# A windowed attention with a gated MLP on one core: idle products on TensorE in the first stages, the rms weights loaded first, batch 0's value copies on POOL

## The chip, the core and the metric

The kernel runs on one core of a Trainium2 chip. The metric is the device time of one execution in microseconds (us). Five engines work side by side, each in order on its own list of instructions, and wait for each other by semaphores: TensorE (PE in the rows, its weight loads PEld), VectorE (DVE), ScalarE (ACT), GpSimd (POOL) and SyncE (SP), which issues most of the DMAs. TensorE reads SBUF and writes PSUM; its clock has two levels, 1.2 and 2.4 GHz, and the rows give the granted share of it as PEclk (0.50 or 1.00).

## The reference

Attention in a window of 64 positions over 8 batches, 8 heads, 576 positions and 64 channels, and then a gated MLP on the 4608 tokens that come out of it (512 channels, 1536 hidden).

```python
scores = matmul(q, k.T) / sqrt(64)          # per batch and head
mask = (rel >= 0) & (rel < 64)              # rel = query position - key position
scores = where(mask, scores, -1e9) - max(...)
attn = exp(scores) / (sum(exp(scores)) + 1e-9)
x = matmul(attn, v)                         # -> 4608 tokens x 512 channels
rms = sqrt(mean(x * x) + 1e-6)
xn = x / rms * rms_g
g, val = xn @ w_gate, xn @ w_val
out = (g * sigmoid(g) * val) @ w_out
```

## The kernel before

*Tiling.* The tokens go through the MLP in 9 tiles of 512; each of the large products is three fp16 products of a high and a low part (`three`, L789 to L792). A batch has 576 tokens, so token tile 0 comes from batch 0 alone, and tile 1 is 64 tokens of batch 0 and 448 of batch 1 (`xn_1`). Heads go in pairs, four to a batch: pairs 0 to 3 are batch 0, 4 to 7 batch 1, and so on.

*Batch 0.* It has its own route in halves of a pair (groups of query blocks, g = 0 and 1). `scores` puts quarters of fp32 products (L386) into PSUM; DVE masks them and takes their row maxima (L399), ACT takes the exponential with its sum (L402), DVE inverts the sums (L469, L470), POOL normalises (L474, L476). `weights_to_keys` transposes the result on TensorE (L489) and copies it out of PSUM, on DVE for one head and on ACT for the other (L492, L494). `attention_values` multiplies by the values (L507). `values_in` loads a pair's values and makes a second copy of them, shifted by a block, with two copies on DVE (L342, L343). Then come squares and their sums (L570 to L575), the root mean square (`tot` L673, the inverse root on DVE L688 to L695), its broadcast by TensorE (`rb` L715), and the normalised tokens `xn` in parts (L740 to L748). `rms_weights` (L172) loads the 512 rms weights, finds their largest with a transposition and a product on TensorE (`gps` L177, `gpb` L181) and scales them by a power of two (L179, L161, L183 to L186).

*Weights.* They come in stages of 1 MB (L192); ACT widens powers of two out of the exponents (L205, L206), TensorE turns these into fp32 scales with the bf16 matrices `unit` of plus and minus one (`pw`, L214, L215, 512 columns), DVE applies them (L217) and finds maxima (L255), and DVE and ACT split into two fp16 parts (L228 to L236).

*Later batches.* From pair 8 on a pair is one piece: masks and exponentials as above into `pm`, 16 moves of rows on POOL (L371, 32 partitions each), and 32x32 transpositions on DVE (L374, L375) in place of those of TensorE.

*What sets the order.* Each engine runs its own list in order. Batch 0 is written as a list of events sorted by a time in half steps (`first_batch`, L627): score, to_keys and values of the eight groups, the root at 10, the weight stages and `rms_weights` at times of a table. All later work is put into a plan of half steps of TensorE (`at_step`). A scheduler with a model of the engines then merges these lists; `tc.issue_after` and `behind` hold a part back until an instruction written ahead of it has been placed. Thus a change of any instruction can shift what is near it in the lists of other engines.

Of the kernel before, what the change touches and what calls it, by code (L numbers as in the profile page):

```python
# [25 lines left out]
P = 128  # L26
# [15 lines left out]
VISITS = (27, 32, 37, 42.5, 47.5)  # L42
MOVES = (8.7, 7, 4.5, 4)
FIRST7 = NT
ORDERED = (1, 3)
PREP0, PREP1 = 32.2, 55.5
ST = 2 * NBLK * P - D
# [9 lines left out]
def tile_window_attention_moe(  # L57
# [54 lines left out]
        nc.vector.tensor_scalar(t[:, 1, :], ident, -1.0, None, ALU.mult)  # L112

    plus_minus(unit)
    one = cp.tile([P, 1], F32, name="one")
    nc.vector.memset(one, 1.0)
    ones = one.to_broadcast([P, P])
# [50 lines left out]
    gmx = cp.tile([P, 2], F32, name="gmx")  # L168
    gex = cp.tile([P, 3], I32, name="gex")
    gpw = cp.tile([P, 2], F32, name="gpw")  # L170

    def rms_weights():  # L172

        nc.sync.dma_start(out=gsb, in_=rms_g)
        nc.vector.tensor_reduce(gmx[:, 0:1], gsb, AX.X, ALU.max, apply_absolute_value=True)
        gps = ps_mi.tile([P, TT], F32, tag="mi", name="gps")
        nc.tensor.transpose(gps[0:1, 0:P], gmx[:, 0:1], ident)  # L177
        nc.vector.tensor_reduce(gmx[0:1, 1:2], gps[0:1, 0:P], AX.X, ALU.max)
        nc.vector.tensor_tensor(gmx[0:1, 1:2], gmx[0:1, 1:2], floor[0:1, :], ALU.max)  # L179
        gpb = ps_mi.tile([P, TT], F32, tag="mi", name="gpb")  # L180
        nc.tensor.matmul(gpb[:, 0:1], lhsT=one[0:1, :].to_broadcast([1, P]), rhs=gmx[0:1, 1:2], start=True, stop=True)  # L181
        exp_bits(gex[:, 0:1], gpb[:, 0:1])
        nc.vector.tensor_scalar(gex[:, 1:2], gex[:, 0:1], 1.0, None, ALU.add)  # L183
        nc.vector.tensor_scalar(gex[:, 2:3], gex[:, 0:1], -1.0, 253.0, ALU.mult, ALU.add)
        pow2(gpw, gex[:, 1:3])
        nc.vector.tensor_scalar(gsb, gsb, gpw[:, 1:2], None, ALU.mult)  # L186
# [139 lines left out]
    def load_kv(n):  # L326

        if n == 3:
            kvt = wk.tile([P, 2, NKD, TT], F16, tag="xn", name=f"kv_{n}")
            kvt = kvt.rearrange("p a b c -> p (a b c)").bitcast(F32)[:, : S + NBLK * P]  # L330
        else:
            kvt = wk.tile([P, S + NBLK * P], F32, tag="kv", name=f"kv_{n}", bufs=NKV)
        if n < NPAIR:
            nc.sync.dma_start(out=kvt[:, :S], in_=kv[n, :, :S])
        else:
            nc.sync.dma_start(out=kvt[:, : S + NKT * P], in_=kv[n])
        even = kvt[:, S : S + NKT * P].rearrange("p (u c) -> p u c", c=P)
        odd = kvt[:, S + NKT * P :].rearrange("p (u c) -> p u c", c=P)

        def values_in():  # L340
            nc.sync.dma_start(out=kvt[:, S : S + NKT * P], in_=kv[n, :, S : S + NKT * P])
            nc.vector.tensor_copy(odd[0:D], even[0:D, : NKT - 1, :])  # L342
            nc.vector.tensor_copy(odd[D:P], even[D:P, 1:, :])  # L343

        if n < NPAIR:
            later[n] = values_in
        else:
            src = kv[n, :, S : S + NKT * P].rearrange("p (u c) -> p u c", c=P)
            nc.sync.dma_start(out=odd[0:D], in_=src[0:D, : NKT - 1, :])
            nc.sync.dma_start(out=odd[D:P], in_=src[D:P, 1:, :])  # L350
        return kvt[:, 0:S], [(odd if j % 2 else even)[:, j // 2, :] for j in range(NBLK)]
# [78 lines left out]

    def scores(n, g, qk):
        qt, kk = qk
        sc, ps = [], []
        for h in range(2):
            if n < NPAIR:
                t = ps_mo.tile([P, TT], F32, tag="mo", name=f"sc_{n}_{g}_{h}")
            elif h == 0:
                t = ps_sc.tile([P, TT], F32, tag="sc", name=f"sc_{n}_{g}_{h}")
            else:
                t = ps_mi.tile([P, TT], F32, tag="mi", name=f"sc_{n}_{g}_{h}")  # L440
            sc.append(t[:, : 3 * P].rearrange("p (i k) -> p i k", i=3))
        for i in range(2):
            for h, par in QUARTERS:
                quarter(sc[h][par * D : (par + 1) * D, i, :], qt, kk, h, 4 * g + 2 * i + 1 + par)
        if g == 0:
            for h in range(2):
                quarter(sc[h][h * D : (h + 1) * D, 2, :D], qt, kk, h, 0)
        part = {}
        for h in range(2):
            p = wk.tile([P, TT], F32, tag="t2k", name=f"p_{n}_{g}_{h}", bufs=T2K)  # L450
            p = p[:, : 3 * P].rearrange("p (i k) -> p i k", i=3)
            ps.append(p)
            for i, u in enumerate(units(g, h)):
                part[u] = p[:, i, :]
        u0, nu = (5, 4) if g else (0, 5)
        st = wk.tile([P, 3, NBLK], F32, tag="st", name=f"st_{n}_{g}", bufs=3)
        for h in range(2):
            for i, u in enumerate(units(g, h)):
                low = st[:, 0, u - u0 : u - u0 + 1]
                if u:  # L460
                    masked(part[u], sc[h][:, i, :], blocked[:, :P], low)
                    continue
                for hh in range(2):
                    hd = slice(hh * D, (hh + 1) * D)
                    masked(part[u][hd, :D], sc[hh][hd, 2, :D], blocked[hd, P:], low[hd])
        for h in range(2):
            for u in units(g, h):
                weigh(part[u][:, : P if u else D], st[:, 0, u - u0 : u - u0 + 1], st[:, 1, u - u0 : u - u0 + 1])
        nc.vector.tensor_scalar(st[:, 1, :nu], st[:, 1, :nu], 1e-9, None, ALU.add)  # L469
        nc.vector.reciprocal(st[:, 2, :nu], st[:, 1, :nu])  # L470
        for h in range(2):
            a = 1 + 4 * g + 2 * h - u0
            r = st[:, 2, a : a + 2].rearrange("p (a b) -> p a b", b=1)
            nc.gpsimd.tensor_tensor(ps[h][:, :2, :], ps[h][:, :2, :], r.to_broadcast([P, 2, P]), ALU.mult)  # L474
            if g == h == 0:
                nc.gpsimd.tensor_tensor(ps[h][:, 2, :D], ps[h][:, 2, :D], st[:, 2, 0:1].to_broadcast([P, D]), ALU.mult)  # L476
        return ps

    def weights_to_keys(n, g, ps):
        pts = []  # L480
        for h in range(2):
            if n < NPAIR and h:
                tr = ps_sc.tile([P, TT], F32, tag="sc", name=f"tr_{n}_{g}_{h}")
            else:
                tr = ps_tr.tile([P, TT], F32, tag="tr", name=f"tr_{n}_{g}_{h}")
            tr = tr[:, : 3 * P].rearrange("p (i q) -> p i q", i=3)
            for i, u in enumerate(units(g, h)):
                w = P if u else D
                nc.tensor.transpose(tr[:w, i, :], ps[h][:, i, :w], ident)  # L489
            pt = pt_pool.tile([P, 3, P], F32, tag="pt", name=f"pt_{n}_{g}_{h}")  # L490
            cpy = nc.scalar.copy if h else nc.vector.tensor_copy
            cpy(pt[:, :2, :], tr[:, :2, :])  # L492
# [5 lines left out]
    def attention_values(n, g, at, vv, xp):  # L498

        xp = xp or x_bank(f"xp_{n}_{g}")  # L500
        for c, j in enumerate(range(5) if g == 0 else range(5, 9)):
            rows = slice(0, P if j else D)
            for h in range(2):
# [8 lines left out]
                    stop=True,  # L512
                    skip_group_check=True,
                )
        return xp

    def attention(b):
# [151 lines left out]
    def inverse_roots(b, ssq):  # L669
        nst = len(starts)  # L670
        tot = ps_mi.tile([P, TT], F32, tag="mi", name=f"tot_{b}")
        for i, a in enumerate(starts):
# [5 lines left out]
                stop=True,  # L678
                skip_group_check=True,
            )  # L680
        rm = wk.tile([P, 3, nst], F32, tag="rm", name=f"rm_{b}")
        m, r, w = (rm[:, i, :] for i in range(3))
        inverse_root(m, r, w, tot[:, :nst])
# [491 lines left out]
```

## Time and profile before

| quantity | value |
|---|---|
| median of 3 runs | 1032.27 us (1031.41 to 1032.70) |
| the profiled execution | 1032.13 us |
| its span from the first to the last instruction | 1030.40 us |
| around the span | 1.73 us |
| busy: PE, PEld | 996.0 us (97%), 499.6 us |
| busy: DVE, ACT, POOL | 479.4, 409.6, 486.5 us |
| matmuls | 6443 |

The rows come from one profiled execution and are read against its own time; times within it start at its first instruction. A row of a timeline groups neighbouring instructions of one line. In a matrix product's row the first shape is the tile of the array (rows used x columns used), the second what it streams. What stands in brackets is the idle time of the engine just before, and what ended it. The program names of a row have their buffer numbers left out in the profile; in the lists of the order they stand in full (`tr_0_1_0` is pair 0, group 1, head 0, and the last number counts buffers).

### The profile page before, as it was taken

What the parts mean: (1) busy time and instruction counts of PE and PEld (TensorE: products, weight loads), DVE (VectorE), ACT (ScalarE), POOL (GpSimd) and SP (SyncE); (2) the same over time, 40 slices, a digit from 0 to 9 for tenths busy, and PEclk for the clock granted to TensorE, in tenths of its full rate; (3) what the DMA queues carried; (4) which work ended last, traced back from release to release, by engine and by line L of the source; (5) the groups of instructions that cost most, each with busy time, mean ns of one, the idle gap of its engine ahead of it and who ended that gap; (6) DMA issues with size and microseconds to landing.
All of it is one profiled execution on the core that took longest, in us unless ns stands there. A gap on an engine that the chain in (4) does not pass through costs nothing.

```text
span 1030.4 us, 16821 instructions
## 1 busy us (share of the span) xinstructions
PE 996.0 (97%) x6443; PEld 499.6 (48%) x6455; DVE 479.4 (47%) x1333; ACT 409.6 (40%) x1066; POOL 486.5 (47%) x634
## 2 busy tenths in 40 slices
PE   7789987999999999999999999999999999999998
PEld 5544544444444445444544454445444444444445
DVE  5688966523374338433743374337533432201220
ACT  5557878234334443334333433443342222212220
POOL 3326644827856576457645764576455022101200
PEclk9989998999999999999999999999999999999999
DMA  7535643011212111211121112111100000000001
GB/s 285 195 107 180 210 158 93 21 35 48 77 57 78 47 47 57 77 47 47 58 77 47 47 57 78 47 47 45 66 2 1 11 31 1 1 21 21 1 1 41
DMA packets 27793, 66.11 MB, mean 64 GB/s; under 512 B 3008, under 2 KB 3264, under 8 KB 27712
## 3 DMA queue, kind: packets, MB, share of 16 engines
q1 hardware_dynamic: 27136, 63.85, 19.1%
q8 instruction: 51, 0.84, 0.3%
q10 hardware_dynamic: 576, 1.18, 0.3%
q14 instruction: 30, 0.25, 0.1%
HBM read 55.58 MB, written 9.44 MB: 63 GB/s over the span
## 4 chain that ended last, share of the span: by engine, by line
PE 84%; DVE 5%; POOL 4%; ACT 4%; DMA 2%; issue 1%; SPq 0%; POOLq 0%; ACTq 0%; DVEq 0%
PE po L791 9%; PE po L792 9%; PE po L790 9%; PE pv L790 8%; PE pg L790 8%; PE pv L792 8%; PE pv L791 8%; PE pg L791 8%; PE pg L792 8%; POOL pm L371 4%; PE sc L386 3%; PE xp L507 2%; PE x L507 2%; DMA kv<-kv 1%; ACT pm L402 1%
## 5 line engine op out<-in xcount | busy, mean ns | idle before, releaser
L371 POOL TENSOR_TENSOR pm<-pm,st 32x288 f32<-32x288 f32 (+1 forms) x384 | 259.1, 675 | 106.9 <-DVE st L428 38.9
L842 POOL TENSOR_TENSOR h<-th,h 128x512 f16<-128x512 f32 x90 | 104.1, 1163 | 175.9 <-ACT h L841 172.7
L839 DVE SCALAR_TENSOR_TENSOR th<-th,pg 128x512 f32<-128x512 f32 x108 | 73.8, 683 | 218.1 <-ACT th L838 218.0
L790 PE MATMUL pv<-xn,wt 128*128 128x512 f16 x432 | 164.9, 382 | 1.9 <-DVE th L839 1.9
L790 PE MATMUL pg<-xn,wt 128*128 128x512 f16 x432 | 164.3, 380 | 1.7 <-ACT wt L235 1.6
L791 PE MATMUL pv<-xn,wt 128*128 128x512 f16 x432 | 164.3, 380 | 0.1
L792 PE MATMUL pv<-xn,wt 128*128 128x512 f16 x432 | 164.2, 380 | 0.1
L791 PE MATMUL po<-wt,h 128*128 128x512 f16 (+1 forms) x436 | 163.5, 375 | 0.8 <-DVE wt L236 0.8
L791 PE MATMUL pg<-xn,wt 128*128 128x512 f16 x432 | 164.0, 380 | 0.0
L792 PE MATMUL pg<-xn,wt 128*128 128x512 f16 x432 | 163.7, 379 | 0.0
L790 PE MATMUL po<-wt,h 128*128 128x512 f16 (+1 forms) x436 | 163.7, 376 | 0.0
L792 PE MATMUL po<-wt,h 128*128 128x512 f16 (+1 forms) x436 | 163.5, 375 | 0.0
L841 ACT CAST h<-th 128x512 f16<-128x512 f32 x105 | 65.0, 619 | 228.2 <-DVE th L840 228.2
L792 PEld LDWEIGHTS <-wt 128*128 128x128 f16 x872 | 85.5, 98 | 102.9 <-issue 1.0
L790 PEld LDWEIGHTS <-wt 128*128 128x128 f16 x872 | 85.4, 98 | 102.5 <-ACT wt L235 1.8
L791 PEld LDWEIGHTS <-wt 128*128 128x128 f16 x872 | 85.7, 98 | 101.6 <-issue 3.2
L838 ACT ACTIVATE th<-pg,hsc 128x512 f32<-128x512 f32 x108 | 74.1, 686 | 102.5 <-PE pg L792 85.1
L840 DVE SCALAR_TENSOR_TENSOR th<-pv,th 128x512 f32<-128x512 f32 x108 | 74.0, 685 | 76.7 <-PE pv L792 76.1
L402 ACT ACTIVATE pm<-pm,st 128x128 f32<-128x128 f32 (+1 forms) x216 | 83.3, 387 | 28.0 <-DVE st L399 27.8
L748 POOL TENSOR_TENSOR xn<-xb,xn 128x64 f16<-128x64 f32 (+7 forms) x63 | 48.9, 806 | 82.7 <-ACT xn L746 82.4
L1003 ACT ACTIVATE ot<-po,hsc 128x512 f32<-128x512 f32 (+1 forms) x37 | 24.9, 674 | 129.3 <-PE po L792 128.9
L792 PEld LDWEIGHTS <-h 128*128 128x128 f16 x436 | 42.9, 98 | 50.0 <-issue 2.1
(144 smaller groups left out, 1090.3 us busy)
## 6 DMA issues: line engine op xcount, KB each, us to landing
kv<-kv SPq DMA_DIRECT2D x28, 608.0 KB, 4.5
out<-ot SPq DMA_DIRECT2D x35, 256.0 KB, 2.0
q<-q SPq DMA_DIRECT2D x28, 288.0 KB, 2.8
kv<-kv SPq DMA_DIRECT2D x56, 128.0 KB, 4.5
st<-w_gate SPq DMA_DIRECT2D x6, 1024.0 KB, 6.4
st<-w_val SPq DMA_DIRECT2D x6, 1024.0 KB, 5.7
st_o<-w_out SPq DMA_DIRECT2D x6, 1024.0 KB, 4.9
kv<-kv SPq DMA_DIRECT2D x4, 320.0 KB, 6.4
```

Of the source, the lines that this page charges most:

```text
L371: nc.gpsimd.tensor_tensor(m[to, :us, fr], p[fr, :us, to], r, ALU.mult)
L402: nc.scalar.activation(part, part, AF.Exp, bias=low, scale=-1.0, accum_out=total)
L507: nc.tensor.matmul(xp[hd, c * D : (c + 1) * D], lhsT=vv[j][rows, hd], rhs=w, start=True, stop=True, skip_group_check=True,)
L748: eng.tensor_tensor(xn[:, 1, kt, o : o + n], x, hi, ALU.subtract)
L790: nc.tensor.matmul(acc, lhsT=lh, rhs=rh, start=first, stop=False)
L791: nc.tensor.matmul(acc, lhsT=lh, rhs=rl, start=False, stop=False)
L792: nc.tensor.matmul(acc, lhsT=ll, rhs=rh, start=False, stop=last)
L838: nc.scalar.activation(th, acc[0], AF.Tanh, scale=th_scale[:, c : c + 1])
L839: nc.vector.scalar_tensor_tensor(th, th, 1.0, acc[0], ALU.add, ALU.mult)
L840: nc.vector.scalar_tensor_tensor(th, acc[1], 2.0**-41, th, ALU.mult, ALU.mult)
L841: (nc.vector.tensor_copy if t < 2 and E('HHE', 'a' * 24)[12 * t + f] == 'v' else nc.scalar.copy)(hh, th)
L842: (nc.vector if t and c == NC - 1 else nc.gpsimd).tensor_tensor(hl, th, hh, ALU.subtract)
```

## The change

1. Directly behind `unit`, 24 products of 128x128 by 256 columns in bf16 go into a PSUM tile that nobody reads (`WARM`).
2. `keep_warm` puts idle products of `unit` into unused columns of a PSUM tile that the real work holds at that time, placed just behind TensorE's last instruction: in batch 0, 6 behind each of the 8 groups' scores, 2 behind each of the 16 sets of transpositions, 4 behind each of the 8 sets of values (128 columns each), and 28 behind `tot` (256 columns).
3. The load of the rms weights moves from SP's queue, in `rms_weights`, to ACT's queue, where it is ACT's first instruction.
4. The two value copies of `values_in` go to POOL. They concern pairs 0 to 3; later pairs get their second copy by DMA.

```diff
--- before.py
+++ after.py
@@ -42,6 +42,7 @@
 VISITS = (27, 32, 37, 42.5, 47.5)
 MOVES = (8.7, 7, 4.5, 4)
 FIRST7 = NT
+WARM, KEEP = 24, (6, 2, 4, 28)
 ORDERED = (1, 3)
 PREP0, PREP1 = 32.2, 55.5
 ST = 2 * NBLK * P - D
@@ -112,6 +113,19 @@
         nc.vector.tensor_scalar(t[:, 1, :], ident, -1.0, None, ALU.mult)
 
     plus_minus(unit)
+
+
+    warm = unit.rearrange("p a b -> p (a b)")
+    idle = ps_mo.tile([P, TT], F32, tag="mo", name="idle")
+    for _ in range(WARM):
+        nc.tensor.matmul(idle[:, : 2 * P], lhsT=warm[:, :P], rhs=warm, start=True, stop=True)
+
+    def keep_warm(cols, times):
+
+        last = next(x for x in reversed(nc.cur_bb.bb.instructions) if x.engine == nc.tensor.engine)
+        with tc.issue_after(last):
+            for _ in range(times):
+                nc.tensor.matmul(cols, lhsT=warm[:, :P], rhs=warm[:, : cols.shape[-1]], start=True, stop=True, skip_group_check=True)
     one = cp.tile([P, 1], F32, name="one")
     nc.vector.memset(one, 1.0)
     ones = one.to_broadcast([P, P])
@@ -168,10 +182,10 @@
     gmx = cp.tile([P, 2], F32, name="gmx")
     gex = cp.tile([P, 3], I32, name="gex")
     gpw = cp.tile([P, 2], F32, name="gpw")
+    nc.scalar.dma_start(out=gsb, in_=rms_g)
 
     def rms_weights():
 
-        nc.sync.dma_start(out=gsb, in_=rms_g)
         nc.vector.tensor_reduce(gmx[:, 0:1], gsb, AX.X, ALU.max, apply_absolute_value=True)
         gps = ps_mi.tile([P, TT], F32, tag="mi", name="gps")
         nc.tensor.transpose(gps[0:1, 0:P], gmx[:, 0:1], ident)
@@ -339,8 +353,8 @@
 
         def values_in():
             nc.sync.dma_start(out=kvt[:, S : S + NKT * P], in_=kv[n, :, S : S + NKT * P])
-            nc.vector.tensor_copy(odd[0:D], even[0:D, : NKT - 1, :])
-            nc.vector.tensor_copy(odd[D:P], even[D:P, 1:, :])
+            nc.gpsimd.tensor_copy(odd[0:D], even[0:D, : NKT - 1, :])
+            nc.gpsimd.tensor_copy(odd[D:P], even[D:P, 1:, :])
 
         if n < NPAIR:
             later[n] = values_in
@@ -430,7 +444,7 @@
 
     def scores(n, g, qk):
         qt, kk = qk
-        sc, ps = [], []
+        sc, ps, banks_of = [], [], []
         for h in range(2):
             if n < NPAIR:
                 t = ps_mo.tile([P, TT], F32, tag="mo", name=f"sc_{n}_{g}_{h}")
@@ -438,6 +452,7 @@
                 t = ps_sc.tile([P, TT], F32, tag="sc", name=f"sc_{n}_{g}_{h}")
             else:
                 t = ps_mi.tile([P, TT], F32, tag="mi", name=f"sc_{n}_{g}_{h}")
+            banks_of.append(t)
             sc.append(t[:, : 3 * P].rearrange("p (i k) -> p i k", i=3))
         for i in range(2):
             for h, par in QUARTERS:
@@ -445,6 +460,8 @@
         if g == 0:
             for h in range(2):
                 quarter(sc[h][h * D : (h + 1) * D, 2, :D], qt, kk, h, 0)
+        if n < NPAIR:
+            keep_warm(banks_of[1][:, 3 * P :], KEEP[0])
         part = {}
         for h in range(2):
             p = wk.tile([P, TT], F32, tag="t2k", name=f"p_{n}_{g}_{h}", bufs=T2K)
@@ -483,10 +500,13 @@
                 tr = ps_sc.tile([P, TT], F32, tag="sc", name=f"tr_{n}_{g}_{h}")
             else:
                 tr = ps_tr.tile([P, TT], F32, tag="tr", name=f"tr_{n}_{g}_{h}")
+            spare = tr[:, 3 * P :]
             tr = tr[:, : 3 * P].rearrange("p (i q) -> p i q", i=3)
             for i, u in enumerate(units(g, h)):
                 w = P if u else D
                 nc.tensor.transpose(tr[:w, i, :], ps[h][:, i, :w], ident)
+            if n < NPAIR:
+                keep_warm(spare, KEEP[1])
             pt = pt_pool.tile([P, 3, P], F32, tag="pt", name=f"pt_{n}_{g}_{h}")
             cpy = nc.scalar.copy if h else nc.vector.tensor_copy
             cpy(pt[:, :2, :], tr[:, :2, :])
@@ -512,6 +532,8 @@
                     stop=True,
                     skip_group_check=True,
                 )
+        if n < NPAIR:
+            keep_warm(xp[:, 3 * P :], KEEP[2])
         return xp
 
     def attention(b):
@@ -678,6 +700,8 @@
                 stop=True,
                 skip_group_check=True,
             )
+        if b == 0:
+            keep_warm(tot[:, 2 * P :], KEEP[3])
         rm = wk.tile([P, 3, nst], F32, tag="rm", name=f"rm_{b}")
         m, r, w = (rm[:, i, :] for i in range(3))
         inverse_root(m, r, w, tot[:, :nst])
```

The lists of the engines show what else moves. Line numbers in the lists of after are 14 to 24 higher than before.

First, TensorE around `gpb`. Before, it stands among the values of pair 0 and the scores of pairs 2 and 3 (`xp_0_1` is pair 0's second group):

```order
L507 MATMUL xp_0_1_354<-pt_0_1_1_301,kv_0_151 64x64
L507 MATMUL xp_0_1_354<-pt_0_1_0_296,kv_0_151 64x64
L507 MATMUL xp_0_1_354<-pt_0_1_1_301,kv_0_151 64x64
L507 MATMUL xp_0_1_354<-pt_0_1_0_296,kv_0_151 64x64
L181 MATMUL gpb_243<-gmx_140,one_109 128x1
L507 MATMUL xp_0_1_354<-pt_0_1_1_301,kv_0_151 64x64
L386 MATMUL sc_3_0_0_473<-kv_3_169,q_3_167 64x128 x3
L489 MATMUL tr_1_1_0_400<-ident_101,p_1_1_0_327 128x128 x2
```

After, the lists of TensorE and, behind it, of DVE. `gpb` follows the scores of pair 2's first half-head and is ahead of the first transposition, `tr_0_0_0`:

```order
L400 MATMUL sc_2_0_0_434<-kv_2_188,q_2_186 64x128 x4
L400 MATMUL sc_2_0_0_434<-kv_2_188,q_2_186 64x64
L191 MATMUL gps_276<-ident_101,gmx_165 1x128
L195 MATMUL gpb_280<-gmx_165,one_134 128x1
L507 MATMUL tr_0_0_0_287<-ident_101,p_0_0_0_225 128x128 x2
L507 MATMUL tr_0_0_0_287<-ident_101,p_0_0_0_225 64x128
L128 LDWEIGHTS unit_106
L128 MATMUL tr_0_0_0_287<-unit_106 128x128
```

On DVE, the step that feeds it (L193) stands behind the sums of pair 1's first group (`st_1_0`, L486):

```order
L486 TENSOR_SCALAR st_0_1_262<-st_0_1_262 128x4
L487 RECIPROCAL st_0_1_262<-st_0_1_262 128x4
L189 TENSOR_REDUCE gmx_165<-gsb_164 128x1
L192 TENSOR_REDUCE gmx_165<-gps_276 1x1
L486 TENSOR_SCALAR st_1_0_323<-st_1_0_323 128x5
L193 TENSOR_TENSOR gmx_165<-gmx_165,floor_136 1x1
L487 RECIPROCAL st_1_0_323<-st_1_0_323 128x5
L175 TENSOR_SCALAR gex_166<-gpb_280 128x1
L197 TENSOR_SCALAR gex_166<-gex_166 128x1
```

The two products moved up past two sets of transpositions and past pair 0's values.

Second, POOL ahead of the first normalisations of batch 0. Before, there is only the CAST of the mask:

```order
L134 AFFINE_SELECT mask_113<-mask_113 64x64 x6
L145 CAST blocked_133<-mask_113 128x192
L474 TENSOR_TENSOR p_0_0_0_193<-p_0_0_0_193,st_0_0_195 128x256
L476 TENSOR_TENSOR p_0_0_0_193<-p_0_0_0_193,st_0_0_195 128x64
L474 TENSOR_TENSOR p_0_0_1_194<-p_0_0_1_194,st_0_0_195 128x256
L474 TENSOR_TENSOR p_0_1_0_222<-p_0_1_0_222,st_0_1_224 128x256
```

After, the value copies of pairs 0, 1 and 2 come ahead, and those of pair 3 behind pair 0's normalisations:

```order
L159 CAST blocked_158<-mask_138 128x192
L356 COPY kv_0_177<-kv_0_177 64x512
L357 COPY kv_0_177<-kv_0_177 64x512
L356 COPY kv_1_181<-kv_1_181 64x512
L357 COPY kv_1_181<-kv_1_181 64x512
L356 COPY kv_2_188<-kv_2_188 64x512
L357 COPY kv_2_188<-kv_2_188 64x512
L491 TENSOR_TENSOR p_0_0_0_225<-p_0_0_0_225,st_0_0_227 128x256
L493 TENSOR_TENSOR p_0_0_0_225<-p_0_0_0_225,st_0_0_227 128x64
L491 TENSOR_TENSOR p_0_0_1_226<-p_0_0_1_226,st_0_0_227 128x256
L491 TENSOR_TENSOR p_0_1_0_260<-p_0_1_0_260,st_0_1_262 128x256
L491 TENSOR_TENSOR p_0_1_1_261<-p_0_1_1_261,st_0_1_262 128x256
```

The normalisation of pair 0 is now seventh behind the CAST instead of first.

Third, later, POOL ahead of token tile 1. Before, the subtractions of `xn_1` (L748) follow pair 9's moves:

```order
L371 TENSOR_TENSOR pm_9_2190<-pm_9_2190,st_9_2191 32x9x32 x8
L371 TENSOR_TENSOR pm_9_2190<-pm_9_2190,st_9_2191 32x8x32 x8
L748 TENSOR_TENSOR xn_1_759<-xb_1_987,xn_1_759 128x448 x4
L748 TENSOR_TENSOR xn_2_2092<-xb_1_987,xn_2_2092 128x128 x4
L842 TENSOR_TENSOR wt18_99<-th_1_0_2238,wt18_99 128x512
L842 TENSOR_TENSOR wt18_99<-th_1_1_2286,wt18_99 128x512
```

After, pair 10's moves are in between:

```order
L385 TENSOR_TENSOR pm_9_2355<-pm_9_2355,st_9_2356 32x9x32 x8
L385 TENSOR_TENSOR pm_9_2355<-pm_9_2355,st_9_2356 32x8x32 x8
L385 TENSOR_TENSOR pm_10_2500<-pm_10_2500,st_10_2501 32x9x32 x8
L385 TENSOR_TENSOR pm_10_2500<-pm_10_2500,st_10_2501 32x8x32 x8
L772 TENSOR_TENSOR xn_1_924<-xb_1_1152,xn_1_924 128x448 x4
L772 TENSOR_TENSOR xn_2_2257<-xb_1_1152,xn_2_2257 128x128 x4
```

Sixteen moves were put ahead of the subtractions. On DVE at the same place, the splits of `w_out` (L236) and pair 8's transposition, before:

```order
L236 SCALAR_TENSOR_TENSOR wt15_96<-wt17_98,hsc_138,wt15_96 128x1024
L694 SCALAR_TENSOR_TENSOR rm_1_1958<-rm_1_1958 128x5
L236 SCALAR_TENSOR_TENSOR wt16_97<-wt18_99,hsc_138,wt16_97 128x1024
L374 STREAM_TRANSPOSE pm_8_1991<-pm_8_1991 128x1024
L695 SCALAR_TENSOR_TENSOR rm_1_1958<-rm_1_1958 128x5
L236 SCALAR_TENSOR_TENSOR wt17_98<-wt19_100,hsc_138,wt17_98 128x1024
```

and after:

```order
L250 SCALAR_TENSOR_TENSOR wt15_96<-wt17_98,hsc_163,wt15_96 128x1024
L388 STREAM_TRANSPOSE pm_8_2156<-pm_8_2156 128x1024
L250 SCALAR_TENSOR_TENSOR wt16_97<-wt18_99,hsc_163,wt16_97 128x1024
L389 STREAM_TRANSPOSE pm_8_2156<-pm_8_2156 64x128
L441 TENSOR_SCALAR st_10_2501<-st_10_2501 128x9
L250 SCALAR_TENSOR_TENSOR wt17_98<-wt19_100,hsc_163,wt17_98 128x1024
```

The transposition of `pm_8` changed places with the split of `wt16`.

## Rows read from the trace of the kernel before

**Rows 1.** Busy time by stretch; columns: stretch, length, engines (instructions), PEclk, DMA, GB/s.

```profile
13.90:36.30 22.40, 22.25 (x173) 15.65 (x173) 13.38 (x77) 14.61 (x53) 8.49 (x16) 1.00 0.55 184
36.30:46.50 10.20, 7.00 (x90) 4.61 (x90) 7.90 (x21) 5.92 (x20) 4.35 (x5) 1.00 0.59 191
46.50:60.10 13.60, 8.49 (x36) 6.45 (x38) 10.57 (x24) 6.48 (x8) 5.59 (x7) 0.50 0.45 143
214.00:1030.00 816.00, 810.03 (x5172) 394.75 (x5170) 333.97 (x878) 273.91 (x742) 379.44 (x492) 1.00 0.13 41
```

**Rows 2.** Timeline of TensorE, 0 to 62; columns: start, duration, instructions, idle before.

```profile
4.87 2.18 PE L386 MATMUL sc<-kv,q 64*64 64x128 f32 x28 [4.87 <-DMA q<-q]
...
25.28 0.58 PE L181 MATMUL gpb<-gmx,one 1*128 1x1 f32 x2
...
35.55 0.61 PE L214 MATMUL pw<-mp,unit 128*128 128x512 bf16 x1
...
37.48 0.38 PE L214 MATMUL pw<-mp,unit 128*128 128x512 bf16 x1
...
47.83 2.29 PE L673 MATMUL tot<-one,ssq 128*128 128x1 f32 x10 [0.42 <-DVE z L267]
54.27 2.05 PE L715 MATMUL rb<-ident,rm 128*128 128x128 f32 x8 [4.15 <-DVE rm L695]
56.11 0.63 PE L214 MATMUL pw<-mp,unit 128*128 128x512 bf16 x1
56.54 0.63 PE L215 MATMUL pw<-mn,unit 128*128 128x512 bf16 x1
```

**Rows 3.** Timeline of DVE, 0 to 62.

```profile
1.63 0.27 DVE L112 TENSOR_SCALAR unit<-ident 128x128 bf16<-128x128 f32 x1
...
8.71 0.29 DVE L399 CUSTOM_DVE_ANT_0 p<-sc,blocked 128x128 f32<-128x128 f32 x1
...
12.65 0.60 DVE L342 COPY kv<-kv 64x512 f32<-64x512 f32 x1
...
21.76 0.61 DVE L179 TENSOR_TENSOR gmx<-gmx,floor 1x1 f32<-1x1 f32 x1
```

**Rows 4.** Groups by line and form, DVE, 0 to 20; busy, mean ns, idle before.

```profile
L343 DVE COPY kv<-kv 64x512 f32<-64x512 f32 x4 | 2.0, 504 | 0.1
```

**Rows 5.** Timeline of ACT, 0 to 62.

```profile
9.04 0.40 ACT L402 ACTIVATE p<-p,st 128x128 f32<-128x128 f32 x1 [5.64 <-DVE st L399]
...
35.63 1.21 ACT L206 ACTIVATE mn<-st,ebias 128x1024 bf16<-128x1024 uint8 x1
```

**Rows 6.** Timeline of POOL, 0 to 62.

```profile
2.92 0.34 POOL L145 CAST blocked<-mask 128x192 bf16<-128x192 f32 x1
12.36 0.61 POOL L474 TENSOR_TENSOR p<-p,st 128x256 f32<-128x256 f32 x1 [9.09 <-ACT p L402]
...
21.74 0.61 POOL L474 TENSOR_TENSOR p<-p,st 128x256 f32<-128x256 f32 x1 [1.72 <-DVE gmx L178]
```

**Rows 7.** Busy time from ACT's first exponential to its last widening, columns as above.

```profile
9.04:36.84 27.80, 27.04 (x217) 19.66 (x218) 18.38 (x108) 19.48 (x76) 10.39 (x18) 1.00 0.62 216
```

**Rows 8.** Timeline of POOL, 172 to 208.

```profile
172.48 16.33 POOL L371 TENSOR_TENSOR pm<-pm,st 32x288 f32<-32x288 f32 x16 [4.20 <-DVE oe L161]
188.89 12.20 POOL L371 TENSOR_TENSOR pm<-pm,st 32x288 f32<-32x288 f32 x16
...
204.00 4.02 POOL L748 TENSOR_TENSOR xn<-xb,xn 128x448 f16<-128x448 f32 x4 [2.92 <-ACT xn L746]
```

**Rows 9.** Timeline of TensorE, 191 to 215.

```profile
191.54 0.38 PE L791 MATMUL po<-wt,h 128*128 128x512 f16 x1 [0.77 <-DVE wt L236]
...
214.13 0.38 PE L790 MATMUL pg<-xn,wt 128*128 128x512 f16 x1
```

**Rows 10.** Timeline of DVE, 188 to 192.

```profile
188.85 1.25 DVE L374 STREAM_TRANSPOSE pm<-pm 128x1024 f32<-128x1024 f32 x1 [3.87 <-POOL pm L371]
190.22 1.27 DVE L236 SCALAR_TENSOR_TENSOR wt<-wt,hsc,wt 128x1024 f16<-128x1024 f32 x1
```

## Prediction

> **What bounds the kernel now.** I read first the table by stage [rows 1]: from 214 to 1030 us TensorE is busy 810.03 of 816.00 at the upper clock. Idle products can return nothing there, and a microsecond won or lost ahead of 214 goes through to the end. So the reader is to look at what lies ahead, the first 60 us above all.
>
> Next TensorE's timeline [rows 2], to be read against the clock column of the table. The column says 1.00 for 13.9 to 36.3, but durations contradict it: a 512-column bf16 product takes 0.61 at 35.55 and 0.38 at 37.48, and 0.63 at 56.11, where the column says 0.50. So TensorE ran at the lower level (1.2 GHz) from its first product to about 36, at the upper (2.4 GHz) until 46.5, and at the lower again from 46.5 to 60.1. In the first stretch it was busy 22.25 of 22.40 us: it set the pace there, with doubled durations. ACT was busy 14.61 of those.
>
> I use the profiled execution, 1032.13 us with a span of 1030.40; the median of the three timed runs is 1032.27, so the forecast is that median plus the sum. A change of 0.2% is 2.06 us, about what a measurement of this kernel can tell from none.
>
> **The change part by part.** *Idle products at the start.* They need only `unit`, ready at 1.63 + 0.27 = 1.90 [rows 3]. One with 256 columns is half of the 512-column rhythm at the lower level, 56.54 - 56.11 = 0.43 [rows 2], so 0.215; 24 make 5.2 and end near 7.0. The first scores, at 4.87 before, are 2.1 late. That also covers the load of the rms weights, now issued ahead of the first queries on ACT's queue: free up to those 2.1. Pair 0's first mask stood at 8.71, behind two value copies of 0.50 [rows 3, 4]; now it waits for scores alone: ten products of 2.18 / 28 = 0.08 [rows 2], 0.4 to 0.8 by the clock, so 7.0 + 0.6 = 7.6, a gain of 1.1.
>
> *The rms weights' two small products.* They were behind pair 0's values (25.28) and now stand ahead of TensorE's first transposition (first pair of order fences). TensorE is in order, so all of batch 0's transpositions wait for a DVE chain that itself stands behind pair 1's sums. Those need 14 exponentials of 0.40 [rows 5]: from 7.6 + 0.3 = 7.9 to 13.5, then L179's counterpart, 0.61 [rows 3], and some 0.3 to the product: TensorE goes on at 14.4. POOL's first block was normalised at 12.36 + 0.61 = 12.97 [rows 6]. So this costs about 1.4, already within the end time worked out below.
>
> L179 is an operation on one element, and its 0.61 is odd. It begins at 21.76, just behind a normalisation on POOL at 21.74, and both take 0.61 [rows 3, 6]. The Trainium skill, "SBUF — State Buffer", section "SBUF: two separate sides", has a rule for that: a VectorE operation with two inputs in SBUF and a GpSimd operation exclude each other, and the later one waits for the whole of the earlier. These two rows agree. By the rule, the step would now wait behind whichever value copy runs on POOL: at most a copy's length instead of 0.61, at least nothing; the sum would move by some half a microsecond at most. I keep the row's 0.61.
>
> *The clock up to 36.84.* At the upper level TensorE's 22.25 become 11.1; the idle products of 128 columns there (by the order 88 of the attention's 112) cost a quarter of 0.215 each, 0.054, together 4.8. Sum 15.9. Then ACT is next. From its first exponential (9.04) to the end of its last widening (35.63 + 1.21 = 36.84) [rows 5] it was busy 19.48 of 27.80 [rows 7]. From 7.9 that gives 27.4 with no wait at all. I allow 4.9 of waits: 2.9 where the masks of pair 1's second group stand behind the rms chain and the first copies out of PSUM, 1.5 where a square stands ahead of pair 3's masks, 0.5 for the rest; they are estimates from the order and DVE's rows. End 32.3, a lead of 4.5. TensorE's 15.9 fit into 32.3 - 14.4 = 17.9, so the idle products are hidden; if the clock doesn't rise they take 88 x 0.107 = 9.4 of path. Bounds of the lead: 0 and 9.4. I take 4.5, nearer to an engine that has waits than to one that has none, since ACT had 8.3 of them before. From 36.84 to 46.5 TensorE was at the upper level already: nothing, give or take 1.
>
> *The root mean square of batch 0.* At the lower level the sums `tot` take 2.29 and the broadcasts `rb` 2.05 [rows 2]. Held up, they take 1.15 and 1.03: 2.2 gained. The 28 idle products between them (0.107 each, 3.0) fit into the 4.15 that TensorE waits for DVE anyway. At the lower level they take 6.0: 1.85 late, and nothing halved.
>
> *Value copies on POOL.* DVE loses the four of L343 at 0.50 [rows 4] and as many of L342, taken alike: 4.0 us; how much of it is a gain is in the steps above. On POOL no row shows a 64x512 copy. From below: DVE's 0.42 to 0.50; from above: the two-input 128x256 at 0.61 [rows 6], twice for the columns, 1.2. I take 0.75, nearer to the CAST of 192 columns in 0.34 [rows 6], twice and a bit. The Trainium skill, "GPSIMD Engine Reference", section 3 (Performance versus the Vector engine), has a simple loop over 512 elements at 769 ns; by that estimate six copies would take 4.6, and the sum would not change. No row here shows it. Six copies stand ahead of the first normalisation (second pair of fences). Pair 0's values are there by 7.7, two copies ahead of 8.71, and pair 2's by 12.65 at the latest, when its first copy ran [rows 3]. The six end at 7.7 + 4.5 = 12.2, or pair 2's at 12.65 + 1.5 = 14.2; with the normalisation, 0.61, that is 12.8 to 14.8. TensorE isn't free for the transposition until 14.4, and I take 0; the cost is up to 1.3 with copies of 1.2.
>
> *What moves later.* In tile 0's weight stages the scheduler's order changes too. POOL now does the 16 row moves of pair 10 ahead of the first subtraction of token tile 1 (third pair of fences). Before: 16 moves from 172.48 in 16.33, 16 in 12.20, the four subtractions at 204.00 in 4.02 [rows 8], done at 208.02 against TensorE's need at 214.13 [rows 9]. Now: 172.48 + 16.33 + 12.20 + 12.20 = 213.2, plus 4.02 = 217.2; the fourth part is needed nine products after 214.13, at half of the 0.43 rhythm each: 216.1. About 1.1 late. On DVE, pair 8's transposition (1.25) now goes ahead of the split of `wt16` (1.27) [rows 10], which released TensorE at 191.54 [rows 9]: up to 1.3 late. These lie on one path, since what is late at 191.5 pushes 214.1 as well; I take 1.5 for both. Bounds: 0, and 5.3 when pair 10's moves go at the slow pace, 16.33 (221.4 against 216.1). All these times move with the lead, so it hides nothing.
>
> Sum: 4.5 + 2.2 - 1.5 = 5.2 gained; 1032.27 - 5.2 = 1027.0.
>
> **The rivals.** A: the clock holds and ACT finds all its inputs in time. 9.4 + 2.2 - 1.5 = 10.1: 1022.0. For it: DVE has 4.0 less to do and TensorE half as much. Against it: 8.3 us of waits before.
>
> B, slower: POOL becomes the bound before token tile 1. Place: L748 behind pair 10's moves; price 5.3 at the slow pace [rows 8]. It decides when the lead is below 5.3. With a clock that falls back in the first stretch the gain is 2.2 alone: 2.2 - 5.3 = -3.1, 1035.4. For it: the first 16 moves took 16.33 and the next 12.20, with nothing changed in their shape. Against: the slow group began with another stage's work beside it.
>
> C: the clock rises at the start, but falls in the pause around the two rms products, when TensorE waits for DVE. Then about half of the stretch runs low: TensorE needs 16.7 for its own work and 7.0 for idle products, 23.7 against 22.25, and the lead is gone. 2.2 - 1.5 = 0.7: 1031.5. For it: TensorE at 22.25 of 22.40 busy did not raise the clock for 22 us, and it rose only with the first 512-column bf16 product near 36. Against it: the idle products are bf16 too.
>
> D, the change doesn't do what it says: idle products never raise the clock. 9.4 + 1.85 + 1.5 slower: 1045.
>
> **How the numbers follow.** Forecast 0.44, A 0.20, C 0.20, B 0.10, D 0.06. The range reaches down past A by its unknown 1 us each side of the stretch after 36.84 (1020.5) and up past C by 2 (1033.5); B and D, 0.16, are left out with a little of A. Forecast and A are faster by over 0.2% (below 1030.2), and a part of C: 0.44 + 0.20 + 0.06 = 0.70. C's rest and little else lies within: 0.14 + 0.02 = 0.16. B and D nearly whole: 0.14.
>
> **What would show it.** Clock: the first scores (0.08 a product before) at half, and the 512-column products at 0.38 from the first. Rms: TensorE's largest gap ending at gpb near 13 to 14.5. Lead: the last widening at 32.3 (27.4 for A, 36.8 for C). Root mean square: `tot` near 1.15, `rb` near 1.03. Later order: the first product of tile 1 against 214.13 minus lead and 2.2, and a wait on L748's counterpart inside its first four. The forecast is wrong if batch 0's TensorE work keeps its duration, or if the lead is there at 46 us and gone at 214.

## The result and the profile after

The changed kernel takes 1041.19 us in the median of 6 runs (1036.14 to 1044.06) against 1031.84 of before (1031.19 to 1032.70, 6 runs): ratio 1.0089, 95% interval 1.0070 to 1.0109. It is slower by 9.4 us, and its own runs differ by 8 us where those of before differ by 1.5: the fastest had a mean granted clock of 0.981, the two slowest 0.975. The profiled run took 1040.17 with a span of 1038.4.

The table by stage of the changed kernel (stretch, length, PE, PEld, DVE, ACT, POOL, PEclk, DMA share, GB/s) answers to [rows 1]:

```profile
6.60:17.00 10.40, 8.27 (x121) 6.53 (x119) 7.48 (x49) 5.39 (x28) 7.87 (x14) 1.00 1.05 393
17.00:30.60 13.60, 13.51 (x109) 10.36 (x110) 5.17 (x38) 8.80 (x33) 3.73 (x9) 0.50 0.36 127
30.60:49.30 18.70, 15.94 (x224) 12.05 (x223) 12.81 (x43) 11.01 (x34) 7.03 (x9) 1.00 0.65 209
49.30:61.90 12.60, 10.25 (x60) 7.38 (x60) 6.35 (x19) 5.81 (x7) 4.22 (x5) 0.73 0.28 93
61.90:223.75 161.85, 147.16 (x952) 75.15 (x951) 114.19 (x318) 106.70 (x241) 91.66 (x114) 0.93 0.38 125
223.75:1036.00 812.25, 808.74 (x5137) 393.80 (x5135) 329.75 (x856) 270.46 (x724) 371.07 (x481) 1.00 0.13 41
```

The borders are marks that both kernels have: the first sum `tot` (49.30; 47.83 before), the first product of token tile 0 (61.91; 59.22) and of tile 1 (223.75; 214.13). Of the 8.0 us between the spans, 1.5 are there at the sums, 1.2 more at tile 0, 6.9 more at tile 1; 1.6 come back behind it. The stretch between the two tiles in the kernel before:

```profile
59.20:214.10 154.90, 142.61 (x908) 72.88 (x917) 108.07 (x295) 103.10 (x222) 85.54 (x101) 0.94 0.39 128
```

Here TensorE is 4.55 us longer busy and 2.4 longer idle after the change. It also has 44 products more in this stretch (952 against 908) and some 35 fewer behind it: a part of the work stood behind tile 1 before, which goes with the 1.6 that come back. TensorE's timeline answers to [rows 2]:

```profile
1.96 5.08 PE L121 MATMUL idle<-unit 128*128 128x256 bf16 x24 [1.96 <-DVE unit L113]
6.97 0.77 PE L400 MATMUL sc<-kv,q 64*64 64x128 f32 x20
...
13.29 0.27 PE L191 MATMUL gps<-ident,gmx 128*1 128x128 f32 x1
14.53 0.38 PE L195 MATMUL gpb<-gmx,one 1*128 1x1 f32 x2 [0.96 <-DVE gmx L193]
...
17.09 0.89 PE L527 MATMUL xp<-pt,kv 64*64 64x64 f32 x6 [1.25 <-DVE pt L514]
...
49.30 1.28 PE L695 MATMUL tot<-one,ssq 128*128 128x1 f32 x10 [0.63 <-DVE z L281]
50.44 4.88 PE L128 MATMUL tot<-unit 128*128 128x256 bf16 x28
57.67 1.84 PE L739 MATMUL rb<-ident,rm 128*128 128x128 f32 x8 [2.35 <-DVE rm L719]
...
89.37 0.61 PE L816 MATMUL pg<-xn,wt 128*128 128x512 f16 x1 [2.54 <-DVE wt L250]
```

The idle products do raise the clock: the first scores take 0.77 for 20, half of before. It falls again at 17.0, behind the two gaps of 0.96 and 1.25 around the rms products, and stays low for 13.6 us (PEclk 0.50, TensorE busy 13.51 of 13.60). And the broadcasts `rb` start 8.4 us behind the first sum, 6.4 before. DVE shows why (these rows answer to [rows 3] and [rows 10]):

```profile
55.36 0.17 DVE L712 TENSOR_SCALAR rm<-tot 128x5 f32<-128x5 f32 x1 [5.05 <-PE tot L128]
...
86.50 2.81 DVE L250 SCALAR_TENSOR_TENSOR wt<-wt,ws,wt 128x1024 f16<-128x1024 f32 x1
```

Its first step on the sums waited 5.05 us, for L128: the idle products, which go into other columns of the tile that it reads. POOL, against [rows 6] and [rows 8]:

```profile
6.93 0.61 POOL L356 COPY kv<-kv 64x512 f32<-64x512 f32 x1 [3.67 <-DMA kv<-kv]
...
86.11 2.13 POOL L244 TENSOR_TENSOR wt<-wt,wt 128x1024 f16<-128x1024 f32 x1 [0.42 <-ACT wt L243]
...
220.02 5.55 POOL L772 TENSOR_TENSOR xn<-xb,xn 128x448 f16<-128x448 f32 x8
```

A value copy takes 0.61. Tile 1's subtractions begin at 220.02 and TensorE comes to them at 223.75 without a gap.

### The profile page after: what moved, and what is told of

It reads as the page before. It is cut to its first block, busy times and chain, and to the rows that moved or that the text cites. A ratio compares the mean times of both kernels' runs of the same rounds, so it can differ in the third digit from the quotient of the medians.

```text
span 1038.4 us, 17152 instructions
## 1 busy us (share of the span) xinstructions
PE 1008.5 (97%) x6619; PEld 508.6 (49%) x6619; DVE 476.3 (46%) x1325; ACT 409.5 (39%) x1066; POOL 488.1 (47%) x642
## 4 chain that ended last, share of the span: by engine, by line
PE 90%; DVE 3%; POOL 3%; ACT 3%; issue 1%; POOLq 0%; ACTq 0%; DVEq 0%
PE po L815 9%; PE po L816 9%; PE po L814 9%; PE pv L814 9%; PE pv L815 8%; PE pv L816 8%; PE pg L816 8%; PE pg L814 8%; PE pg L815 8%; PE sc L400 3%; PE xp L527 2%; POOL pm L385 2%; PE x L527 2%; PE tr L507 1%; DVE wt L250 1%
```

## The experiments

Each ratio is to the kernel before, timed on the same chip; e14 and e15 are one run each. Times within a run are from its profile; the medians vary with the clock, so both are given. POOL's later list shows two forms: in the form of before, 32 row moves run in one go ahead of tile 1's subtractions (also e2, e4 to e9, e11, e16); in the form of the changed kernel it is 48, with pair 10's (also e1, e3, e10, e12, e13).

| run | first sum | first product of tile 0 | from there to tile 1 | median, us |
|---|---|---|---|---|
| before | 47.83 | 59.22 | 154.9 | 1031.84 |
| changed | 49.30 | 61.91 | 161.8 | 1041.19 |
| e1 no idle products | 42.31 | 53.70 | 162.4 | 1034.61 |
| e2 28 in own tile | 46.26 | 54.66 | 157.3 | 1031.77 |
| e3 without the 28 | 50.45 | 60.14 | 157.3 | 1034.91 |
| e4 rms load on SP | 55.32 | 67.93 | 156.4 | 1043.90 |
| e5 only 28, own tile | 41.73 | 51.50 | 156.8 | 1026.92 |
| e6 all, own tile, rms later | 42.36 | 52.40 | 157.1 | 1027.68 |
| e7 only 28, own tile, rms later | 41.28 | 51.33 | 157.2 | 1026.28 |
| e8 only copies on POOL | 48.53 | 59.08 | 156.7 | 1032.91 |
| e9 as e7, tile that is read | 41.60 | 55.68 | 159.4 | 1029.91 |
| e10 as e7, no idle products | 41.05 | 52.43 | 162.6 | 1033.55 |
| e11 as e7, 12 at the start | 41.52 | 51.57 | 156.9 | 1026.18 |
| e12 only rms load first | 43.90 | 55.27 | 162.6 | 1036.64 |
| e13 changed, rms later | 42.74 | 56.97 | 163.0 | 1036.87 |
| e14, e15 changed again | 51.03, 49.35 | 63.62, 61.91 | 161.9, 161.4 | 1041.93, 1041.16 (one each) |
| e16 as e7 with 24 | 41.49 | 50.75 | 157.1 | 1026.54 |

**e1.** `WARM, KEEP = 0, (0, 0, 0, 0)` in the changed kernel.

> The change without any idle product (rms weights first and value copies on POOL stay). The lists of the engines from batch 1 on are nearly those of the changed kernel. Theory (three costs: the order of the later stages, readers that wait for idle products in their PSUM tile, a clock that falls in the pause around the rms products): the first 60 us as before within 1 us, first product of tile 0 near 59 to 60, then 4 to 6 us lost on the way to 214 as in the changed kernel; 1036 to 1037. Rival (idle products cost it all): 1031 to 1032.5.

Measured 1034.61, ratio 1.0025 (1.0016 to 1.0035). Theory and rival both missed the front: without any idle product it is 5.5 us shorter than before, not equal. So the rms load and the copies bring a lead, the idle products cost 8.2 on top of it (61.91 against 53.70), and the stretch to tile 1 loses 7.5 without them too. The total lies between the two ranges.

**e2.** The 28 in their own tile:

```diff
-            keep_warm(tot[:, 2 * P :], KEEP[3])
+            keep_warm(ps_tr.tile([P, TT], F32, tag="tr", name="idle2")[:, 2 * P :], KEEP[3])
```

> The changed kernel with the 28 idle products behind the sums of squares in a PSUM tile of their own instead of in spare columns of the tile that DVE reads. The lists of later stages come out nearly as before. Theory: DVE reads the sums 0.1 to 0.2 us after the last of the ten sum products, not 4.8 us later; the broadcasts start near 53 to 55 (57.67 in the changed kernel, 54.27 before); with the later order of before 1030 to 1033. Rival (DVE's chain is late for another reason, and the tile costs nothing): broadcasts still near 57.5, 1036 or more.

1031.77, ratio 1.0007 (0.9993 to 1.0021), broadcasts at 52.12, 5.9 behind the first sum. The total is the theory's. The broadcasts come ahead of its 53 to 55, since the first sum was itself 3.0 earlier than in the changed kernel, with the clock low for 6.8 us instead of 13.6; and the order of the later stages changed too. So e9 is the cleaner test.

**e3.** `KEEP = (6, 2, 4, 0)`.

> The changed kernel without the 28 idle products behind the sums of squares. Theory: the broadcasts start at 53 to 55; if the order of later stages costs as in the changed kernel, 1035 to 1037, else 1031 to 1033. Rival (the 28 products were worth their place, since they held the clock for the broadcasts): broadcasts at twice their duration and later than 57, 1040.

1034.91, ratio 1.0029 (1.0018 to 1.0041). The broadcasts start 5.4 behind the first sum, but that sum was late (50.45): in this profile the clock was low from about 15 to 35. They ran at the lower clock (2.04), as the rival said, but not later than 57; the total lies just under the theory's first range. POOL's list has the 48 moves ahead of tile 1's subtractions here as well, and the stretch to tile 1 is 157.3 all the same: these moves are not what the later order costs.

**e4.** The load of the rms weights on SP's queue again, inside `rms_weights`, as before; all else changed.

> The changed kernel with the load of the rms weights on SP's queue as before. The second small product then follows the first transpositions instead of standing ahead of them. Theory: TensorE's gap ahead of that product (0.96) and the following 1.25 shrink; the clock stays up past 17 for some us; the 28 idle products still hold DVE for near 5 us; 1033 to 1036. Rival (the fall at 17 has nothing to do with the rms products): the clock falls at the same place, 1036 to 1040.

1043.90, ratio 1.0126 (1.0111 to 1.0140): theory and rival both missed it. TensorE's timeline in e4:

```profile
12.26 0.76 PE L399 MATMUL sc<-kv,q 64*64 64x128 f32 x10
19.68 0.37 PE L190 MATMUL gps<-ident,gmx 128*1 128x128 f32 x1 [6.66 <-DVE gmx L188]
```

The first rms product still stands ahead of all transpositions. Its load, issued at 8.2, lands 11.2 us later, DVE's first step on it waits 5.57 for that, and TensorE 6.66 for DVE.

**e5, e7, e10, e11, e16.** No idle products in the attention. e5 is e2 with `WARM, KEEP = 0, (0, 0, 0, 28)`; e7 is e5 with `rms_weights` at time 4 instead of 2 in batch 0's list of events, where its entry is `r`:

```diff
-'r': 2,
+'r': 4,
```

> Of the idle products only the 28 behind the sums of squares, in a PSUM tile of their own; rms weights first and value copies on POOL as in the change. The lists of later stages come out in the form of before (the first experiment had that of the changed kernel). Theory (idle products in batch 0's attention only lengthen TensorE's work while the clock is low; the order of later stages is a cost of its own): front as in the first experiment, first product of tile 0 near 53 to 54.5 (59.22 before, 61.90 changed), and most of this lead still there at 214; 1026 to 1029. Rival (the lead is given back in any order, since weights come no earlier): first product near 54, but 1031 to 1033.

> As e5 but with the rms weights' steps at time 4 instead of 2. Theory: front like e5 or up to 1 us better, since nothing of the rms chain stands ahead of the first copies out of PSUM; 1025 to 1029. Rival (the early place of the rms chain was what sped the front up): first product of tile 0 near 57 to 59, 1029 to 1032.

e5 1026.92, ratio 0.9963 (0.9951 to 0.9975); e7 1026.28, ratio 0.9948 (0.9936 to 0.9960). Both totals are the theory's. In e5 the first product of tile 0 came at 51.50, ahead of the theory's 53 to 54.5; e7 is there as forecast.

e10 is e7 with no idle product at all, which also turns the later lists into the changed kernel's form:

> As e7 without the 28 idle products: no idle product at all, rms steps at time 4, value copies on POOL. The lists of later stages come out in the form of the changed kernel. Theory (order of later stages costs 5 to 7 us by itself): the sums start near 41.3 as in e7, the first product of tile 0 some 11.4 behind them (10.05 in e7), and 161 to 163 us from there to the first product of tile 1 (157.2 in e7): 1032 to 1035. Rival (the order costs nothing, and the other runs lost time through the clock): 1027 to 1028.

1033.55, ratio 1.0020 (1.0010 to 1.0030), within the theory's range, and its three other numbers are met too. The stretches from tile 0 to tile 1, first of e7, then of e10:

```profile
51.30:208.50 157.20, 145.01 (x918) 73.27 (x917) 110.44 (x297) 104.16 (x224) 85.50 (x102) 0.96 0.38 127
```

```profile
52.40:215.00 162.60, 144.85 (x941) 74.51 (x951) 113.79 (x317) 106.43 (x240) 91.94 (x113) 0.96 0.37 124
```

TensorE is as long busy at the same clock, and idle 17.8 instead of 12.2: 5.4 lost, by waits. It isn't the lack of the 28 products that makes them: e3 and e8 lack them as well, and take 157.3 and 156.7. So it is the order; which exchange in it costs the time is not shown, only that it isn't pair 10's moves (e3).

e11 adds `WARM = 12` to e7, e16 has 24 products in place of 28:

> As e7 with 12 idle products of 256 columns at the start. Lists of later stages as in e7. Theory (the front is not bound by TensorE's clock once the rms products and the copies are out of the way): the clock is up from about 5, first product of tile 0 at 51 to 52.5 as in e7, 1026 to 1028. Rival (an early rise of the clock is worth the 12 us at the low level in e7): first product of tile 0 at 46 to 49, 1021 to 1024.

> As e7 with 24 products instead of 28 in their own tile; lists otherwise as e7. In e7 DVE's inverse root was done at 47.57 and the broadcasts started at 48.78, behind the idle products. Theory: the broadcasts start 0.5 to 0.9 us earlier, 1025.4 to 1026.3. Rival (with fewer products the clock isn't up for the broadcasts): first product of tile 0 1 to 2 us later, 1027 to 1028.

e11 1026.18, ratio 0.9949 (0.9936 to 0.9962): nothing gained, but not for the reason given. The 12 products did not raise the clock; products have the lower level's length until 21.5, in e7 until 17.3 (and once more from 27.8 to 31). e16 1026.54, ratio 0.9959 (0.9948 to 0.9971): broadcasts 0.6 earlier, as expected; the total lies between the two ranges and within the spread of e7 (1025.25 to 1026.69).

**e6, e13, e14, e15.** All idle products. e6 is e2 with the rms steps at time 4; e13 is the changed kernel with that alone.

> All idle products (the 28 in a tile of their own), but the rms weights' steps moved from time 2 to 4 in the list of events, so that both small products stand behind pair 0's first values on TensorE. Theory (the pause around the rms products at 13.6 to 17.1 lets the clock fall, and only at the low level do the idle products cost): TensorE has no gap of over 0.6 us between 7 and 40, the clock stays up from 7 to 45, first product of tile 0 near 50 to 53, 1024 to 1028. Rival (the clock falls near 17 anyway, since TensorE waits for the first normalised block and its copies): a low stretch of 7 to 20 us from 17 on, 1027 to 1037 like the second experiment.

> The changed kernel with only the rms weights' steps moved from time 2 to 4 in the list of events; the 28 products stay in the tile that DVE reads, POOL's list is the same. Theory (the pause around the rms products lets the clock fall, and at the low level the idle products lengthen the front): clock up from about 5 to past 40, sums start near 42 to 43 (49.30 changed), first product of tile 0 at 54 to 57; then 161 to 163 to tile 1; 1034 to 1037. Rival (the clock falls at 17 anyway): sums near 46 to 50, 1039 to 1043.

e6 1027.68, ratio 0.9980 (0.9953 to 1.0007). Ten of its 12 runs took 1026.1 to 1029.8 at a mean granted clock of 0.988 to 0.991; one took 1037.47 at 0.980 and one 1041.46 at 0.975. Total and first product of tile 0 (52.40) are the theory's. e13 1036.87, ratio 1.0056 (1.0044 to 1.0068), first sum at 42.74 instead of 49.30, with the same list on POOL; all its numbers are the theory's. The stretch of e6, then of e13, that answers to the low one of the changed kernel:

```profile
17.00:30.60 13.60, 13.60 (x185) 10.62 (x183) 7.50 (x47) 11.40 (x36) 6.42 (x13) 1.00 0.65 207
17.00:30.60 13.60, 13.60 (x187) 10.68 (x184) 8.39 (x50) 11.40 (x37) 8.14 (x15) 1.00 0.64 201
```

185 and 187 products instead of 109 in the same time, at 1.00. With the rms products later the clock stays up, and that is worth 6.6 us at the first sum (e13). Without idle products in the attention the same move is worth 0.4 (41.73 in e5, 41.28 in e7), so nearly all of the 6.6 is what the idle products cost at the lower clock, not the wait itself. And e7, with no idle product ahead of the sums and the lower clock until 17.3, is at its first sum at 41.28, before e6 (42.36): holding the clock up to there bought nothing that wasn't to be had without.

> The changed kernel, one more profile. Theory (its times differ by the length of the low stretch that begins near 17): each 3.4 us of that stretch more or less moves the first product of tile 0 by 1.5 to 2.5 us in the same direction (61.90 with 13.6 us in the first profile). Rival (the spread comes from later stages): the first product of tile 0 within 1 us of 61.9 and the difference behind it.

> The changed kernel, a third profile, with what is expected of the second: a longer low stretch and a later first product of tile 0 together, or, by the rival, a first product within 1 us of 61.9.

e14: low from about 15 to 36, 6.8 longer than in the first profile, and the first product of tile 0 1.7 later, where 3 to 5 was expected; e15: the same stretch and the same 61.91, and 1 us more lost behind tile 0. That one lies behind tile 1: around 294 its clock was low for 3.4 us (PEclk 0.86 from 290 to 302, 1.00 in the first profile). The runs that have the same attention show the low stretch's price: 6.8 us of it and a first sum at 46.26 (e2), 13.6 and 49.30 and 49.35 (changed, e15), 20.5 and 50.45 and 51.03 (e3, e14). So it is a part of the spread of 8 us, and low stretches further on are another.

**e8, e12.** One part alone.

> The kernel before with only the value copies on POOL; no idle products, rms weights as before. Lists of later stages in the form of before. Theory (the copies taken from DVE are what brings the front forward, by letting masks and exponentials run earlier): first product of tile 0 near 54 to 56; 1027 to 1030. Rival (the front is bound by TensorE at the low clock, copies or not): first product near 58.5 to 59.5, 1031 to 1032.

> The kernel before with only the load of the rms weights moved to the head of ACT's queue; copies on DVE, no idle products. The lists of later stages come out in the form of the changed kernel. Theory (both parts are needed for the shorter front: the rms weights in time, so that TensorE's small product doesn't wait, and DVE freed of copies): first product of tile 0 at 56 to 59, then 161 to 163 us to tile 1; 1034 to 1038. Rival (the rms load alone brings the front): first product of tile 0 at 53 to 55; 1031 to 1034.

e8 1032.91, ratio 1.0015 (1.0007 to 1.0024): the theory fell. Copies on POOL alone leave the front as it was (59.08), as the rival had it; the total is a little above the rival's. e12 1036.64, ratio 1.0057 (1.0040 to 1.0075): the rms load alone brings the front forward by 4.0, between what theory and rival said, and turns the later order into the changed kernel's form; the total is the theory's. The copies add 1.6 to that lead (e1 against e12) and nothing without it (e8).

**e9.** As e7, but `keep_warm(tot[:, 2 * P :], 28)`: the only difference is the tile.

> As e7, but the 28 idle products in the spare columns of the tile with the sums of squares, as in the change. Same lists otherwise. Theory (DVE waits for the last product into the tile that it reads): DVE's first step behind the sums starts 4.8 to 6 us after the last sum instead of at once, the broadcasts start 9 to 11 us after the first sum (7.5 in e7), 1028 to 1030. Rival (the tile doesn't matter): as e7, 1025.5 to 1027.

1029.91, ratio 0.9985 (0.9972 to 0.9998), against 1026.28 and 0.9948 of e7; the theory's numbers are all met. TensorE and DVE of e7:

```profile
41.28 2.29 PE L695 MATMUL tot<-one,ssq 128*128 128x1 f32 x10 [0.63 <-DVE z L281]
43.43 5.51 PE L128 MATMUL idle<-unit 128*128 128x256 bf16 x28
48.78 1.06 PE L739 MATMUL rb<-ident,rm 128*128 128x128 f32 x8
```

```profile
43.61 0.16 DVE L712 TENSOR_SCALAR rm<-tot 128x5 f32<-128x5 f32 x1 [1.31 <-PE tot L695]
43.80 1.99 DVE L713 TENSOR_SCALAR rm<-rm 128x5 int32<-128x5 int32 x1
```

and of e9:

```profile
43.76 5.31 PE L128 MATMUL tot<-unit 128*128 128x256 bf16 x28
51.41 1.98 PE L739 MATMUL rb<-ident,rm 128*128 128x128 f32 x8 [2.35 <-DVE rm L719]
```

```profile
49.10 0.16 DVE L712 TENSOR_SCALAR rm<-tot 128x5 f32<-128x5 f32 x1 [6.50 <-PE tot L128]
```

In e7 DVE reads at once and works beside the idle products; the broadcasts behind them run at the upper clock (1.06). In e9 DVE starts when they end, TensorE then waits for DVE, and the clock is down again for the broadcasts (1.98). First product of tile 0: 51.33 and 55.68. From the first sum to there it is 10.05 in e7, 14.08 in e9 and 11.38 in e10, which has no idle product: the 28 gain 1.3 in a tile of their own and lose 2.7 in the tile that is read. (e9's profile loses 2.2 more up to tile 1; there its clock was low for some 7 us longer than in e7.)

## Why the prediction was wrong

It said 1027.0 and at most 1033.5; 1041.19 was measured. The sum was 5.2 gained, the profile lost 8.0. Three terms make up the difference of 13.2:

- **"The 28 idle products between them (0.107 each, 3.0) fit into the 4.15 that TensorE waits for DVE anyway"** (2.2 gained). This step failed in kind. DVE's wait (5.05) is for the last product into the tile, so the products are not beside the chain but ahead of it, and they took 4.88 and not 3.0; from the first sum to tile 0 the profile lost 1.2: 3.4 off. e9 against e7 shows it with nothing else changed: 4.3 us at tile 0, 3.6 in the medians. The diff shows the place: `keep_warm(tot[...])` stands ahead of `inverse_root(..., tot[...])`. Even in a tile of their own the 28 gained 1.3 and not 2.2 (e7 against e10).
- **The lead of 4.5 up to 36.84.** The first sum came 1.5 late: 6.0 off. The gap that rival C named was there at its place (TensorE went on at 14.53, forecast 14.4) and the clock fell behind it. What the prediction held against that rival, that the idle products are bf16 too, did not hold. Nor was its price right: it took the loss as the lead alone, though its own working had TensorE 1.4 longer (23.7 against 22.25). e13 puts the place of the rms products, with the idle products there, at 6.6 us at the first sum.
- **The later order, 1.5 lost.** It was 5.3 (6.9 up to tile 1, 1.6 back): 3.8 off. The place was wrong too. At tile 1 TensorE did not wait for POOL at all (223.75), so neither the term nor rival B was at work. The 6.9 are 2.4 more of waits, which lie between 74 and 200, such as the 2.5 for the split L250 at 89.37; up to 3 from more time at the lower clock (some 24 us low instead of 18, summed from PEclk in steps of 1 us); and the work that moved ahead of tile 1. e10 against e7 prices the order at 5.4 up to tile 1, by waits, with TensorE's busy time and clock unchanged.

Right were the start (idle products to 7.04, forecast 7.0; first mask at 7.89, forecast 7.6), the time at which TensorE is free for transpositions, and that the copies on POOL cost nothing there (0.61 each; 0.75 was taken, where the CAST's row gives 0.91 by columns). The lower end of the range, 1020.5, isn't the 1022.0 less 1 that it is said to be; nothing hangs on it. But the reading under it all was half wrong: TensorE busy 22.25 of 22.40 at the lower clock was taken as what the idle products must cure. e1, e5, e7 and e10 have no idle product in the attention, and the clock rises between 17 and 24 all the same; their first sum is 5.5 to 6.8 earlier than before. Rival D ("idle products never raise the clock") is refuted for 24 of them and was seen for 12 (e11).

What stays open: why the clock rises at 17 to 24.5 in the runs with the rms load first and no idle products in the attention, and at about 36 to 39 in the two with that load late and none (before, e8); and so whether the earlier front of these runs comes from the clock or from the rms weights being there in time. Why the low stretch of the changed kernel is of different length from run to run. And which part of the later order makes the waits.

The version to keep is e7: value copies on POOL, rms load first but its two products behind the first values, and the 28 products in a tile of their own: 1026.28, some 5 us (0.52%) faster than before. e11 and e16 are within its spread.

## What to carry to other kernels

An idle product is ordered like any other: look at which tile it writes, who reads that tile, and whether the reader waits for the last writer. Idle time of one engine is not free room if the engine that ends it has to wait for what is put there. Before paying for a higher clock, see whether TensorE is what the next stage waits for at that clock; and in a kernel whose order comes from a scheduler, time the new order by itself, since an edit of a few instructions early in the program moved the later stages by 5 us here.

## What had not been expected of the hardware

A split on DVE that elsewhere takes 1.27 or 1.28 took 2.81 (86.50, above) while POOL worked from 86.11 to 88.24, and TensorE waited 2.54 for it. A 128x5 step that takes 0.17 in e9 took 1.99 in e7 (43.80 to 45.79), beside a POOL operation of 2.13 that ended at 45.76. The first agrees with the rule of the Trainium skill, "SBUF — State Buffer", section "SBUF: two separate sides", by which a VectorE operation with two inputs in SBUF waits for the whole of a GpSimd operation that began earlier: both inputs of the split are in SBUF. The second has one small input; that POOL held it up is what the times suggest, and no run tests it. The prediction used the rule for half a microsecond on one step and did not look for it in the splits.
